# Attention with top-32 selection and an MLP on one core: engines of small copies and the planner's priorities chosen anew

## The chip, the cores and the metric

The kernel runs on one NeuronCore of a Trainium2 chip. The metric is the time of one execution on the device, in microseconds (us), as the median of several runs. The core has five engines with a queue of instructions each: TensorE (PE, matmuls; its weight loads are shown as PEld), VectorE (DVE), ScalarE (ACT), GpSimd (POOL) and SyncE (SP), which here issues all DMAs. An instruction waits in its queue until the semaphores it names have been reached, and what stands behind it waits too.

## The reference

Four batches of eight heads attend over 576 positions; of each row of scores only the 32 largest are kept. The result, as 2304 rows of 512, goes through a matmul to 2048, softplus, and a matmul back to 512.

```python
scores = scale * np.matmul(q, k.transpose(0, 1, 3, 2))
kth = np.partition(scores, -top_k, axis=-1)[..., -top_k:-top_k + 1]
scores = np.where(scores >= kth, scores, -1000000000.0)
attn = softmax(scores)                       # with 1e-09 added to the sum
x = np.matmul(attn, v)                       # heads side by side: 2304 x 512
h = x @ w_in                                 # 512 x 2048
g = np.maximum(h, 0.0) + np.log1p(np.exp(-np.abs(h)))
out = g @ w_out                              # 2048 x 512
```

`w_in` and `w_out` come as 64-bit floats. The kernel splits each of them on the chip into a high and a low float32 part, and runs the matmuls of the MLP with three products (high x high, high x low, low x high).

## The kernel before

**Work and stages.** Heads go in pairs. A batch is cut into two ranges of 256 rows and a remainder of 64 (two heads' remainders share a tile). A step of the sequence is a head pair of one range: for each of two tiles of 128 rows, scores by TensorE (`qk`, line 582), a copy from PSUM by ScalarE (`copy`, lines 680 and 695), then the selection: maxima of eight chunks (`c8`, line 623), three rounds of maxima (`m8`, lines 632 and 638), a count of what lies above (`cnt` on VectorE, line 654, or `sign` and `relu` on ScalarE, lines 648 and 651), products by POOL (`z`, lines 657 and 660) and a last maximum (`w8`, line 662). Then the exponential (`exp`, line 720), the mask with its sum (`mask`, line 723), transposes (`T`, line 738), their copies (`evac`, line 743) and attention times v (`av`, line 783). At the end of a step the row factors are spread out to a tile `rr` (`WIDES`: line 800 on VectorE, 797 on ScalarE, 794 on POOL), and the result is split into a high and a low part x (`xh` on ScalarE, line 822, or `xsplit` on POOL, lines 825 and 828; `X_HIGHS`).

**The MLP** (called MoE in the names) runs over nine blocks of 256 rows, each when its range is done (the remainders of all batches make the ninth), in eight units of two feature tiles. A unit is 24 matmuls of line 915 in PSUM (`moeh`), |h| (line 928), exponential and logarithm on ScalarE (934, 936), the addition on VectorE (`g`, line 942) or on POOL (`gs`, line 939, with a Relu on ScalarE before it), the high part of g (ScalarE, `gh`, line 945, or POOL, `gs`, line 948; `HIGHS`), the low part on POOL (`gs`, line 950) and 12 matmuls of line 960 (`moeo`). The low part of w_in lies in DRAM and is loaded for each tile (`wl`); `wl` is also the class of the output's stores.

**Weights** are prepared in 32 pieces of 128 x 512 in eight parts of four (a part of w_in, then one of w_out, four times): a load of 512 KB (`wload`) to one of two staging buffers, |w| on ScalarE (lines 432 and 446), four steps on VectorE (434 to 442 for the first 20 pieces, whose temporaries lie in PSUM; 449 to 460 for the others, whose clamp is on POOL or on VectorE by `POOL_CLAMPS`), the high part (ScalarE, line 470, or POOL, line 467, by `POOL_HIGHS`), and the low part on POOL (475 and 486). Only pieces from 20 on look at `POOL_CLAMPS`. Five parts come first in the sequence, parts 5 and 6 ahead of the first unit of the first block of the MoE, part 7 ahead of its fourth. The temporaries of a piece and of a unit come from the same ring `a` of two buffers, which are given out in the order of the program. q and k are split on POOL (`split`, lines 503 and 506), turned on TensorE (`prepT`, line 513) and copied on ScalarE (`prepev`, lines 538 and 566), three stages ahead (`AHEAD`).

**Order.** No queue's order is written out by hand. Each piece of work is an `Op` with an engine, a cost, what it depends on, buffers that it takes or frees, and a priority: its place in the sequence (0 to 72 for the steps, 1.5 more for each unit within the MoE) plus an offset from `OFFS`, chosen by its class and by which of four stages its place falls in (below 5.5, 11.5, 60.5, or above). `Plan.forward` goes through the work in time: of the instructions of an engine whose inputs are planned it takes the one that can start first, and among those that could start at the same time the lowest priority. The queues are filled in the order of the starts so found. The places in the sequence span some 80, so offsets that lie further apart than this rank classes whatever their place.

```python
if k in OFFS:
    prio += OFFS[k][sum(prio >= s for s in STAGES)]
```

Of the kernel before, what the change touches and what calls it, by code (L numbers as in the profile page):

```python
# [16 lines left out]
LOW = -3.0e38  # L17
LARGEST = 3.0e38
COUNTS = tuple(map(int, "101111011111111010000010100000000001000000100000010000000001110001111100"))
POOL_CLAMPS = (0, 1, 11, 12, 13, 16, 22, 27, 28, 29, 30)  # L20
POOL_HIGHS = (16, 20, 27, 28)
AHEAD = 3
WIDES = tuple(map(int, "20200000010022000000011110212002"))
GUARDS = (1,)
SPLITS = tuple(map(int, "000000001101110101101000001010110001001100000101101111100010100111000100"))
REST_LAST = (0, 0, 0, 0)
HIGHS = tuple(map(int, "011101011111001100011000011001100010000010011100110110100010101111111001"))
X_HIGHS = tuple(map(int, "000011101000001000011011000011011100"))
W_AT = (-1, -1, -1, -1, -1, 0, 0, 3)
EARLY_PIECES = 20  # L30
EARLY_PAIRS = 8
# [2 lines left out]
PASSES = 0  # L34
SLOPE = 1.5
STAGES = (5.5, 11.5, 60.5)
OFFS = {"T": (-291.57, -322.01, -530.19, -242.94,),
        "av": (-276.33, -303.72, -359.32, -241.06,),
        "c8": (380.01, 363.38, 650.87, 238.59,),
        "cnt": (459.77, 102.79, 428.38, 267.79,),  # L40
        "copy": (563.64, 134.42, 465.54, 349.87,),
        "evac": (-215.5, 195.29, 114.86, -425.45,),
        "exp": (384.13, 367.5, 654.99, 185.69,),
        "g": (459.85, 106.18, 431.76, 267.87,),
        "gh": (157.89, 1.42, -29.55, 2.84,),
        "gs": (-41.02, 199.82, 518.18, 316.26,),
        "guard": (460.45, 92.47, 425.27, 268.16,),
        "inv": (-313.3, -9.08, 77.16, 53.56,),
        "load": (-308.68, -253.81, -285.11, -120.84,),
        "loadv": (-111.81, -2.43, 0.31, -5.31,),  # L50
        "m8": (464.05, 628.42, 662.54, 681.81,),
        "mask": (-279.8, 144.17, 122.8, -287.92,),
        "moeh": (-110.15, -1.19, 1.29, 0.7,),
        "moeo": (-230.73, -31.51, 4.57, 4.37,),
        "neg": (-358.45, -475.13, -56.27, -387.03,),
        "prepT": (-312.78, -270.79, -357.79, -176.61,),
        "prepev": (-284.19, 126.51, 55.57, -348.47,),
        "qk": (148.36, 42.76, 0.24, 1.21,),
        "rb": (655.1, 219.15, 591.6, 419.43,),
        "relu": (558.22, 134.9, 425.49, 532.22,),  # L60
        "sign": (-317.65, -268.47, -359.67, -138.32,),
        "soft": (-44.66, 199.71, 542.61, 328.67,),
        "split": (-170.82, 264.58, 203.08, -458.5,),
        "w8": (385.5, 675.11, 522.15, 411.57,),
        "wl": (-291.21, -321.65, -529.83, -242.58,),
        "wload": (-241.23, -34.37, -0.49, 20.42,),
        "wprep": (-299.35, -227.01, -273.63, -218.46,),
        "xh": (567.18, 145.59, 586.57, 538.21,),
        "xsplit": (-342.34, -259.25, -284.47, -149.07,),
        "z": (-254.7, -227.33, -283.53, -305.94,)}  # L70
BIG = 2.0 ** 40
TIERS = (2, 6, 8)
CHUNKS = 8
# [73 lines left out]
class Plan:  # L147
# [7 lines left out]
    def add(self, eng, cost, fn, deps=(), acq=(), rel=(), prio=0.0, lat=0.0, k=None, port=False):  # L155
        if k in OFFS:
            prio += OFFS[k][sum(prio >= s for s in STAGES)]
        op = Op(eng, cost, fn, list(deps), list(acq), list(rel), prio, lat, len(self.ops),
                port or eng == "pool")
        self.ops.append(op)  # L160
        return op
# [127 lines left out]
def c_act(n, psum=False, ptr=0):  # L289
    return (120 if psum else 162) + 0.714 * n + 93 * ptr  # L290
# [10 lines left out]
def c_pool(n, scalar=False):  # L301
    return 155 + 0.834 * n if scalar else 150 + 2.15 * n
# [3 lines left out]
def topk_attention_moe(ctx: ExitStack, tc: tile.TileContext, q, k, v, w_in, w_out, out):  # L306
# [83 lines left out]
    def add(*args, **kw):  # L390
        return pl.add(*args, **kw)
# [13 lines left out]
    def prep_weights(part, prio):  # L405

        group, which = divmod(part, 2)
        for j in range(4):
# [13 lines left out]
            def high(st=st):  # L422
                return st.ap().rearrange("p (c t) -> p c t", t=2)[:, :, 1]
# [21 lines left out]
            else:  # L445
                ab = add("act", c_act(512) + 45, lambda high=high, tm=tm: nc.scalar.activation(
                    tm.ap(), high().bitcast(F32), AF.Abs), [ld], acq=[tm], prio=prio, k="wprep")
                if piece in POOL_CLAMPS:
                    a0 = add("pool", c_pool(512, True), lambda tm=tm: nc.gpsimd.tensor_scalar(
# [14 lines left out]
            if fast and piece == EARLY_PIECES - 1:  # L464
                add("dve", 0, lambda: None, last_words[-2:], rel=lent[:1], prio=prio, k="g")
            if piece in POOL_HIGHS:
                oh = add("pool", c_pool(512, True), lambda tm=tm, hi=hi: nc.gpsimd.tensor_scalar(
# [290 lines left out]
    def full_range(b, r, hp, qt, qops, kt, kops, vt, vops, seq, last_k):  # L758
# [32 lines left out]
        wide = lambda: sums.ap()[:, 0:4].unsqueeze(2).to_broadcast([P, 4, D])  # L791
        how = WIDES[next(range_no) % len(WIDES)]
        if how == 2:
# [26 lines left out]
    def split_x(x, src, dep, rel, key, hp, prio):  # L820
        if X_HIGHS[next(x_no) % len(X_HIGHS)]:
            h = add("act", c_act(CH), lambda: nc.scalar.activation(x.ap()[:, 0, :], src(), AF.Copy), dep, acq=[x], prio=prio, k="xh")
        else:
            h = add("pool", c_pool(CH, True),
                    lambda: nc.gpsimd.tensor_scalar(x.ap()[:, 0, :], src(), 1.0, 0.0, op0=OP.mult, op1=OP.add), dep, acq=[x],
                    prio=prio, k="xsplit")
        l = add("pool", c_pool(CH),
                lambda: nc.gpsimd.tensor_tensor(x.ap()[:, 1, :], src(), x.ap()[:, 0, :].bitcast(F32), op=OP.subtract),
                [h], rel=rel, prio=prio, k="xsplit")
        xu.setdefault(key, {})[hp] = (x, [h, l])  # L830
# [63 lines left out]
    def moe(key, seq, first):  # L894
# [4 lines left out]
        for s in range(KF // 2):  # L899
# [41 lines left out]
            else:  # L941
                o4 = add("dve", c_dve(512), lambda hb=hb, ab=ab: nc.vector.scalar_tensor_tensor(  # L942
                    ab.ap(), hb.ap(), 0.0, ab.ap(), op0=OP.max, op1=OP.add), [o3], rel=[hb], prio=prio, k="g")
            if HIGHS[unit % len(HIGHS)] and fast:
                g1 = add("act", c_act(512), lambda ab=ab, gb=gb: nc.scalar.activation(gb.ap()[:, 0, :], ab.ap(), AF.Copy),  # L945
# [176 lines left out]
```

## Time and profile before

| | |
|---|---|
| median of 3 runs | 855.11 us (854.74 to 856.41) |
| profiled execution | 853.7 us, span 851.7 us |
| mean granted TensorE clock | 0.954 of full speed |
| busy: PE, PEld, DVE | 89%, 77%, 82% of the span |
| busy: ACT, POOL | 73%, 72% of the span |

Busy shares are means over the whole span, which has stretches with different limits; so the tables by stretch say more. Matmuls are pipelined, so a busy PE is not PE at its peak. The span is that of the instructions; the execution has 2.0 us beside it.

### The profile page before, as it was taken

The numbers are of one execution on the slowest core, as the hardware profiler recorded it, in microseconds if no ns is written. First come the engines' busy times: TensorE is split into PE (matmuls) and PEld (weight loads), VectorE is DVE, ScalarE is ACT, GpSimd is POOL, SyncE is SP. The second block draws the span as 40 slices with busy tenths as digits, with TensorE's granted clock in tenths as the row PEclk, the third lists the DMA queues.
The fourth block names the chain that finished last, engine by engine and source line by source line (L and its number), as shares of the span: only waits on it lengthen the run. The fifth ranks groups of instructions, "written<-read, shape, count | busy, mean of one in ns | idle before, by whom it ended". The sixth has DMA issues, their size and how long they took to land.

```text
span 851.7 us, 18516 instructions
## 1 busy us (share of the span) xinstructions
PE 757.8 (89%) x5894; PEld 658.9 (77%) x5894; DVE 696.3 (82%) x3095; ACT 620.1 (73%) x1196; POOL 613.5 (72%) x817
## 2 busy tenths in 40 slices
PE   2466558698989999999999999999999999999996
PEld 1354447587879898988798889887988898898885
DVE  4999988989998899888998998899987966855000
ACT  3787668889869985877687858866888688955442
POOL 3786557878879987788897775799878558846341
PEclk9986756899999999999999999999999999999999
DMA  7655344623334322424243224242422151051331
GB/s 223 210 143 184 118 127 131 183 84 115 90 95 112 97 71 76 125 68 115 72 126 82 69 69 123 65 114 80 132 82 63 51 137 49 28 162 55 89 93 42
DMA packets 66763, 88.34 MB, mean 104 GB/s; under 512 B 12640, under 2 KB 37216, under 8 KB 66656
## 3 DMA queue, kind: packets, MB, share of 16 engines
q1 hardware_dynamic: 66656, 87.06, 35.6%
q8 instruction: 49, 0.80, 0.4%
q14 instruction: 58, 0.48, 0.2%
HBM read 68.68 MB, written 8.91 MB: 91 GB/s over the span
## 4 chain that ended last, share of the span: by engine, by line
PE 44%; DVE 24%; POOL 14%; ACT 11%; issue 5%; DMA 1%; ACTq 0%; POOLq 0%; DVEq 0%
PE ps L960 14%; PE ps L915 14%; DVE c L623 6%; PE ps L582 6%; POOL z L660 4%; PE ps L783 4%; PE ps L738 4%; DVE kth L662 3%; DVE sg L654 2%; DVE c L638 2%; DVE l L632 2%; POOL g L950 2%; POOL z L657 2%; POOL hl L506 2%; ACT sg L648 2%
## 5 line engine op out<-in xcount | busy, mean ns | idle before, releaser
L960 PE MATMUL ps<-woh,g 128*128 128x512 f32 x576 | 212.6, 409 | 1.4 <-POOL g L950 1.4
L660 POOL TENSOR_TENSOR z<-s,sg 128x576 f32<-128x576 f32 x144 | 194.8, 1353 | 1.0
L623 DVE MAX8 c<-s 128x8 f32<-128x72 f32 x1152 | 168.2, 219 | 30.9 <-ACT s L680 27.7
L915 PE MATMUL ps<-x,wih 128*128 128x256 f32 x1152 | 176.3, 289 | 1.5 <-DVE a L942 1.4
L915 PEld LDWEIGHTS ps<-x,wih 128*128 128x128 f32 x1152 | 152.6, 191 | 5.3 <-DVE a L942 1.8
L582 PE MATMUL ps<-kt,qt 128*128 128x288 f32 (+2 forms) x672 | 132.5, 325 | 9.8 <-ACT s L680 5.3
L743 ACT ACTIVATE et<-ps 128x512 f32<-128x512 f32 (+1 forms) x208 | 103.4, 497 | 45.5 <-PE ps L738 44.7
L662 DVE MAX8 kth<-z 128x8 f32<-128x584 f32 x144 | 109.8, 762 | 23.3 <-POOL z L660 22.4
L960 PEld LDWEIGHTS ps<-woh,g 128*128 128x128 f32 x576 | 108.7, 189 | 23.3 <-POOL g L950 2.5
L582 PEld LDWEIGHTS ps<-kt,qt 128*128 128x128 f32 x672 | 104.3, 205 | 20.6 <-ACT s L680 8.5
L950 POOL TENSOR_TENSOR g<-a,g 128x512 fp32r<-128x512 f32 x72 | 94.9, 1318 | 33.7 <-ACT g L945 31.9
L960 PE MATMUL ps<-wol,g 128*128 128x512 f32 x288 | 113.8, 395 | 0.0
L657 POOL TENSOR_SCALAR z<-small,stats 128x8 f32<-128x8 f32 x144 | 66.0, 458 | 63.4 <-DVE kth L662 29.3
L680 ACT ACTIVATE s<-ps 128x576 f32<-128x576 f32 x128 | 83.2, 650 | 29.0 <-PE ps L582 22.2
L738 PE MATMUL ps<-identr,em 128*128 128x128 f32 x392 | 73.5, 299 | 32.7 <-DVE em L723 17.2
L915 PE MATMUL ps<-x,wil 128*128 128x256 f32 x576 | 95.0, 287 | 0.0
L783 PE MATMUL ps<-et,vt 128*64 128x128 f32 x1280 | 91.6, 294 | 0.0
L738 PEld LDWEIGHTS ps<-identr,em 128*128 128x128 f32 x392 | 50.3, 151 | 46.3 <-ACT et L743 11.0
L783 PEld LDWEIGHTS ps<-et,vt 128*64 128x64 f32 x1280 | 75.1, 146 | 12.6 <-issue 6.8
L915 PEld LDWEIGHTS ps<-x,wil 128*128 128x128 f32 x576 | 78.3, 190 | 0.5 <-issue 0.2
L632 DVE MAX8 l<-c 128x8 f32<-128x64 f32 (+2 forms) x432 | 75.1, 197 | 2.7
L513 PE MATMUL ps<-identr,hl 128*128 128x128 f32 x288 | 40.9, 264 | 35.9 <-POOL hl L506 22.6
(102 smaller groups left out, 1461.1 us busy)
## 6 DMA issues: line engine op xcount, KB each, us to landing
wil<-wil_d SPq DMA_DIRECT2D x144, 256.0 KB, 2.9
qt<-qt SPq DMA_DIRECT2D x72, 128.0 KB, 2.7
shared<-in_moe_w_in_dram SPq DMA_DIRECT2D x16, 512.0 KB, 3.7
shared<-in_moe_w_out_dram SPq DMA_DIRECT2D x16, 512.0 KB, 3.6
nat<-in_q_dram SPq DMA_DIRECT2D x32, 128.0 KB, 2.2
nat<-in_k_dram SPq DMA_DIRECT2D x32, 128.0 KB, 2.2
vt<-in_v_dram SPq DMA_DIRECT2D x16, 256.0 KB, 2.8
wil_d<-g SPq DMA_DIRECT2D x16, 256.0 KB, 2.6
```

Of the source, the lines that this page charges most:

```text
L582: nc.tensor.matmul(sp.ap()[:, c:c + w], qt.ap()[:, a, ti, :], kt.ap()[:, kc:kc + w], start=(a == 0), stop=(a == 1))
L623: nc.vector.max(out=ct[i].ap()[:, 8 * c:8 * c + 8], in_=v[:, c, :])
L632: last[i] = add("dve", c_max(w * CHUNKS), lambda i=i, rnd=rnd, part=part: nc.vector.max(out=lt.ap()[:, i, rnd, :], in_=part(i)), [last[i]] ...
L660: b = add("pool", 150 + 1.92 * S, lambda i=i, sg=sg, z=z: nc.gpsimd.tensor_tensor(z.ap()[:, 0:S], sc[i].ap(), sg.ap(), op=OP.mult), [f], r ...
L662: w = add("dve", c_max(S + 8), lambda z=z, top8=top8: nc.vector.max(out=kth[:, top8:top8 + 8], in_=z.ap()), [b, *order8], rel=[z], prio=pr ...
L680: lambda i=i, sp=sp: nc.scalar.activation(sc[i].ap(), sp.ap(), AF.Copy, scale=scale),
L738: nc.tensor.transpose(tr.ap()[:, j * P:(j + 1) * P], em.ap()[:, c0 + j * P:c0 + (j + 1) * P], ident)
L743: lambda: nc.scalar.activation(et.ap()[:, b0:b0 + n, :].rearrange("p a c -> p (a c)"), tr.ap()[:, 0:n * P], AF.Copy),
L783: nc.tensor.matmul(o[hh * D:(hh + 1) * D, :], vt.ap()[:, hh * NT + j if j < NT else 2 * NT + hh, :], et.ap()[:, hh * NT + j if j < NT else ...
L915: nc.tensor.matmul(o, w, units[kk][0].ap()[:, c, :], start=(n == 0 and kk == 0), stop=(n == 2 and kk == KD - 1))
L950: g2 = add("pool", c_pool(512), lambda ab=ab, gb=gb: nc.gpsimd.tensor_tensor(gb.ap()[:, 1, :], ab.ap(), gb.ap()[:, 0, :].bitcast(F32), op= ...
L960: nc.tensor.matmul(o, gb.ap()[:, a, c:c + P], w[:, f, :], start=(f == 0 and n == 0), stop=(f == KF - 1 and n == 2))
```

## The change

Five tuples that choose engines and the whole table of offsets get new values; no function changes. The choices take effect as follows (counts of the whole program):

| | before | after |
|---|---|---|
| clamps on POOL (pieces 20 to 31) | 22, 27, 28, 29, 30 | 22, 27, 28, 29, 31 |
| high parts of weights on POOL | 16, 20, 27, 28 | 1, 3, 4, 9, 10, 11, 20, 27, 28 |
| row factors on VectorE, ScalarE, POOL | 19, 6, 7 | 17, 7, 8 |
| high parts of g on ScalarE, POOL | 37, 35 | 41, 31 |
| high parts of x on ScalarE, POOL | 14, 22 | 16, 20 |

```diff
-POOL_CLAMPS = (0, 1, 11, 12, 13, 16, 22, 27, 28, 29, 30)
-POOL_HIGHS = (16, 20, 27, 28)
+POOL_CLAMPS = (22, 27, 28, 29, 31)
+POOL_HIGHS = (1, 3, 4, 9, 10, 11, 20, 27, 28)
-WIDES = tuple(map(int, "20200000010022000000011110212002"))
+WIDES = tuple(map(int, "20100020021001201022022000011010"))
-HIGHS = tuple(map(int, "011101011111001100011000011001100010000010011100110110100010101111111001"))
-X_HIGHS = tuple(map(int, "000011101000001000011011000011011100"))
+HIGHS = tuple(map(int, "011111011111001101111000011101110111001010010001000110001111010011010110"))
+X_HIGHS = tuple(map(int, "000011001010101000110011001101111000"))
...
-        "T": (-291.57, -322.01, -530.19, -242.94,),
-        "av": (-276.33, -303.72, -359.32, -241.06,),
-        "c8": (380.01, 363.38, 650.87, 238.59,),
-        "cnt": (459.77, 102.79, 428.38, 267.79,),
-        "copy": (563.64, 134.42, 465.54, 349.87,),
-        "g": (459.85, 106.18, 431.76, 267.87,),
-        "gh": (157.89, 1.42, -29.55, 2.84,),
-        "gs": (-41.02, 199.82, 518.18, 316.26,),
-        "inv": (-313.3, -9.08, 77.16, 53.56,),
-        "load": (-308.68, -253.81, -285.11, -120.84,),
-        "m8": (464.05, 628.42, 662.54, 681.81,),
-        "mask": (-279.8, 144.17, 122.8, -287.92,),
-        "moeh": (-110.15, -1.19, 1.29, 0.7,),
-        "moeo": (-230.73, -31.51, 4.57, 4.37,),
-        "prepT": (-312.78, -270.79, -357.79, -176.61,),
-        "qk": (148.36, 42.76, 0.24, 1.21,),
-        "sign": (-317.65, -268.47, -359.67, -138.32,),
-        "split": (-170.82, 264.58, 203.08, -458.5,),
-        "w8": (385.5, 675.11, 522.15, 411.57,),
-        "wl": (-291.21, -321.65, -529.83, -242.58,),
-        "wload": (-241.23, -34.37, -0.49, 20.42,),
-        "wprep": (-299.35, -227.01, -273.63, -218.46,),
-        "z": (-254.7, -227.33, -283.53, -305.94,)}
+        "T": (-324.15, -345.9, -530.65, -319.11,),
+        "av": (-283.14, -289.79, -359.32, -240.73,),
+        "c8": (406.4, 359.15, 653.29, 262.28,),
+        "cnt": (521.83, 10.31, 421.74, 347.32,),
+        "copy": (580.5, 206.37, 407.71, 326.96,),
+        "g": (536.69, 125.2, 439.85, 385.76,),
+        "gh": (-323.83, -332.81, -365.08, -317.16,),
+        "gs": (440.87, 44.94, 326.47, 178.74,),
+        "inv": (36.81, -88.7, 1.71, -2.55,),
+        "load": (-329.04, -335.29, -359.72, -311.3,),
+        "m8": (524.23, 619.11, 683.88, 660.36,),
+        "mask": (437.66, 81.52, 333.44, 239.57,),
+        "moeh": (-90.39, -42.08, 1.41, 0.85,),
+        "moeo": (-233.07, -22.11, 4.55, 5.15,),
+        "prepT": (-338.79, -273.83, -357.71, -180.91,),
+        "qk": (38.7, -114.5, 0.19, 1.72,),
+        "sign": (-303.77, -237.88, -269.33, -166.3,),
+        "split": (508.2, 71.67, 403.94, 306.36,),
+        "w8": (437.85, 661.49, 450.91, 377.0,),
+        "wl": (-312.15, -449.72, 1.58, -357.77,),
+        "wload": (-1.83, -106.33, -125.62, -70.92,),
+        "wprep": (-299.76, -225.91, -284.63, -249.65,),
+        "z": (-308.89, -226.26, -272.88, -254.56,)}
...
```

The classes left out (`evac`, `exp`, `guard`, `loadv`, `neg`, `prepev`, `rb`, `relu`, `soft`, `xh`, `xsplit`) get new values too.

## Rows read from the trace of the kernel before

**Rows 1.** The head of the profile's page.
```profile
span 851.7 us, 18516 instructions
```

**Rows 2.** Busy time by stretch (from:to, length, engines with counts, granted clock, DMA).
```profile
core 0: us, PE busy (x) PEld busy (x) DVE busy (x) ACT busy (x) POOL busy (x), PEclk, DMA share, GB/s
...
25.00:125.00 100.00, 57.09 (x327) 44.77 (x328) 96.91 (x376) 73.33 (x141) 69.96 (x104) 0.74 0.54 163
125.00:200.00 75.00, 58.97 (x463) 50.58 (x461) 67.11 (x267) 63.45 (x125) 57.41 (x65) 0.86 0.44 132
200.00:675.00 475.00, 464.79 (x3835) 408.52 (x3835) 439.05 (x2073) 364.42 (x709) 383.24 (x526) 1.00 0.32 89
675.00:800.00 125.00, 124.31 (x963) 109.54 (x963) 75.90 (x315) 88.46 (x172) 78.81 (x93) 1.00 0.29 81
800.00:845.00 45.00, 44.84 (x285) 39.76 (x283) 3.46 (x5) 20.08 (x34) 15.77 (x14) 1.00 0.32 90
```

**Rows 3.** Busy time up to 200 us, of line 915 and then of line 960.
```profile
0.00:200.00 200.00, 18.95 (x120) 17.33 (x120) 0.82 0.52 156
...
0.00:200.00 200.00, 9.86 (x36) 6.37 (x36) 0.82 0.52 156
```

**Rows 4.** The chain of work that ended last (start, us, what), near its end.
```profile
825.32 2.80 PE ps L960 x12
828.12 2.80 PE ps L915 x24
```

**Rows 5.** VectorE's waits, 200 to 675 us (total, times, longest).
```profile
DVE c L623 <- ACT s L680: 11.2, 8, 3.2
DVE kth L662 <- POOL z L660: 9.1, 16, 2.1
```

**Rows 6.** Timeline 120 to 174 us (start, us, engine, line): TensorE, POOL, ScalarE, VectorE, TensorE.
```profile
140.68 1.73 PE L915 MATMUL ps<-x,wih 128*128 128x256 f32 x8
...
160.20 1.60 POOL L475 TENSOR_TENSOR g<-a,wih 128x512 fp32r<-128x512 f32 x1
...
162.33 0.58 ACT L928 ACTIVATE a<-ps 128x512 f32<-128x512 f32 x1
...
162.28 0.81 DVE L723 SCALAR_TENSOR_TENSOR em<-s,kth,em 128x576 f32<-128x576 f32 x1
...
172.22 0.48 PE L960 MATMUL ps<-woh,g 128*128 128x512 f32 x1
```

**Rows 7.** Timeline 44 to 57 us: one weight piece, and the load that follows it.
```profile
44.81 0.33 SPq L397 DMA_DIRECT2D shared<-in_moe_w_in_dram  x1
...
50.09 0.65 ACT L432 ACTIVATE ps<-shared 128x512 f32<-128x512 f32 x1
...
54.78 0.67 DVE L442 SCALAR_TENSOR_TENSOR a<-shared,ps 128x512 uint32<-128x512 uint32 x1
...
56.30 0.46 SPq L397 DMA_DIRECT2D shared<-in_moe_w_in_dram  x1
```

**Rows 8.** Groups by line (count, busy us, mean ns, idle before): copies that change engines.
```profile
L470 ACT ACTIVATE wih<-a 128x512 fp32r<-128x512 f32 x14 | 8.8, 629 | 11.1 <-DVE a L442 10.4 <-DVE a L460 0.6
...
L467 POOL TENSOR_SCALAR woh<-a 128x512 fp32r<-128x512 f32 x2 | 1.3, 670 | 2.3 <-DVE a L460 2.3
...
L945 ACT ACTIVATE g<-a 128x512 fp32r<-128x512 f32 x37 | 23.3, 630 | 10.6 <-PE ps L960 5.6 <-POOL a L939 3.7 <-DVE a L942 1.1
...
L948 POOL TENSOR_SCALAR g<-a 128x512 fp32r<-128x512 f32 x35 | 21.8, 623 | 10.2 <-PE ps L960 6.8 <-DVE a L942 2.4 <-PE ps L513 0.5
...
L800 DVE COPY rr<-sum 128x256 f32<-128x256 f32 x19 | 8.3, 436 | 0.1
```

**Rows 9.** Groups by line: the MoE's additions and low parts on POOL.
```profile
L950 POOL TENSOR_TENSOR g<-a,g 128x512 fp32r<-128x512 f32 x72 | 94.9, 1318 | 33.7 <-ACT g L945 31.9
...
L939 POOL TENSOR_TENSOR a<-shared,a 128x512 f32<-128x512 f32 x30 | 39.2, 1308 | 25.6 <-ACT a L936 25.5
```

**Rows 10.** VectorE steps of weight pieces: line 454 (ns min/median/max), line 436 (as rows 8).
```profile
L454 DVE TENSOR_SCALAR a<-a x12: 409/423/1417, 116.1 to 200.0; 128x512 uint32<-128x512 uint32 x12
...
L436 DVE TENSOR_SCALAR ps<-ps 128x512 uint32<-128x512 uint32 x20 | 13.8, 691 | 0.1
```

More of the change, by code (lines that the diff above doesn't have):

```diff
@@ L36 @@
 STAGES = (5.5, 11.5, 60.5)
-OFFS = {"T": (-291.57, -322.01, -530.19, -242.94,),
-        "av": (-276.33, -303.72, -359.32, -241.06,),
-        "c8": (380.01, 363.38, 650.87, 238.59,),
-        "cnt": (459.77, 102.79, 428.38, 267.79,),
-        "copy": (563.64, 134.42, 465.54, 349.87,),
-        "evac": (-215.5, 195.29, 114.86, -425.45,),
-        "exp": (384.13, 367.5, 654.99, 185.69,),
-        "g": (459.85, 106.18, 431.76, 267.87,),
-        "gh": (157.89, 1.42, -29.55, 2.84,),
-        "gs": (-41.02, 199.82, 518.18, 316.26,),
-        "guard": (460.45, 92.47, 425.27, 268.16,),
-        "inv": (-313.3, -9.08, 77.16, 53.56,),
-        "load": (-308.68, -253.81, -285.11, -120.84,),
-        "loadv": (-111.81, -2.43, 0.31, -5.31,),
-        "m8": (464.05, 628.42, 662.54, 681.81,),
-        "mask": (-279.8, 144.17, 122.8, -287.92,),
-        "moeh": (-110.15, -1.19, 1.29, 0.7,),
-        "moeo": (-230.73, -31.51, 4.57, 4.37,),
-        "neg": (-358.45, -475.13, -56.27, -387.03,),
-        "prepT": (-312.78, -270.79, -357.79, -176.61,),
-        "prepev": (-284.19, 126.51, 55.57, -348.47,),
-        "qk": (148.36, 42.76, 0.24, 1.21,),
-        "rb": (655.1, 219.15, 591.6, 419.43,),
-        "relu": (558.22, 134.9, 425.49, 532.22,),
-        "sign": (-317.65, -268.47, -359.67, -138.32,),
-        "soft": (-44.66, 199.71, 542.61, 328.67,),
-        "split": (-170.82, 264.58, 203.08, -458.5,),
-        "w8": (385.5, 675.11, 522.15, 411.57,),
-        "wl": (-291.21, -321.65, -529.83, -242.58,),
-        "wload": (-241.23, -34.37, -0.49, 20.42,),
-        "wprep": (-299.35, -227.01, -273.63, -218.46,),
-        "xh": (567.18, 145.59, 586.57, 538.21,),
-        "xsplit": (-342.34, -259.25, -284.47, -149.07,),
-        "z": (-254.7, -227.33, -283.53, -305.94,)}
@@ new lines @@
+OFFS = {"T": (-324.15, -345.9, -530.65, -319.11,),
+        "av": (-283.14, -289.79, -359.32, -240.73,),
+        "c8": (406.4, 359.15, 653.29, 262.28,),
+        "cnt": (521.83, 10.31, 421.74, 347.32,),
+        "copy": (580.5, 206.37, 407.71, 326.96,),
+        "evac": (-193.99, 216.59, 63.92, -437.06,),
+        "exp": (319.52, 363.16, 721.52, 184.84,),
+        "g": (536.69, 125.2, 439.85, 385.76,),
+        "gh": (-323.83, -332.81, -365.08, -317.16,),
+        "gs": (440.87, 44.94, 326.47, 178.74,),
+        "guard": (1.22, -144.33, -13.98, 25.92,),
+        "inv": (36.81, -88.7, 1.71, -2.55,),
+        "load": (-329.04, -335.29, -359.72, -311.3,),
+        "loadv": (475.88, 82.77, 353.11, 217.11,),
+        "m8": (524.23, 619.11, 683.88, 660.36,),
+        "mask": (437.66, 81.52, 333.44, 239.57,),
+        "moeh": (-90.39, -42.08, 1.41, 0.85,),
+        "moeo": (-233.07, -22.11, 4.55, 5.15,),
+        "neg": (-321.23, -484.49, -18.09, -311.87,),
+        "prepT": (-338.79, -273.83, -357.71, -180.91,),
+        "prepev": (7.86, -43.1, 64.37, 33.81,),
+        "qk": (38.7, -114.5, 0.19, 1.72,),
+        "rb": (603.54, 239.36, 666.58, 472.35,),
+        "relu": (602.35, 107.29, 388.15, 537.0,),
+        "sign": (-303.77, -237.88, -269.33, -166.3,),
+        "soft": (-62.58, 234.2, 580.81, 317.04,),
+        "split": (508.2, 71.67, 403.94, 306.36,),
[3 more added lines that the diff above has]
+        "wprep": (-299.76, -225.91, -284.63, -249.65,),
+        "xh": (547.37, 123.93, 616.24, 613.36,),
+        "xsplit": (-296.71, -231.74, -269.12, -231.45,),
+        "z": (-308.89, -226.26, -272.88, -254.56,)}
```

## The prediction

> **What bounds the kernel now.** I read the stretches first. The table of busy time by stretch has three parts [rows 2]. From 25 to 125 us VectorE is busy 96.91 of 100 us and TensorE 57.09, at a granted clock of 0.74: the start belongs to VectorE, which does the top-32 search and the bit work on the weights at once. From 200 to 675 us both are nearly full, TensorE 464.79 and VectorE 439.05 of 475 us, at clock 1.00. From 675 on TensorE is alone: 124.31 of 125 us and 44.84 of 45, while VectorE falls to 75.90 and 3.46. The span is 851.7 us [rows 1].
>
> So the end is set by TensorE's backlog of MoE matmuls. In the last steps a MoE unit takes 2.80 us for 12 matmuls of line 960 and 2.80 us for 24 of line 915 [rows 4]. That is 0.233 us and 0.117 us each, so 864 and 1728 of them (9 blocks of 16 feature tiles, 6 and 12 matmuls per tile) come to 201.6 us each, 403 us together. Before 200 us only 36 and 120 have run [rows 3], 8.4 + 14.0 = 22.4 us. The other 381 us must fit behind 200 us, beside attention. A microsecond by which the MoE starts earlier, or a TensorE hole closed after 200 us, is worth up to a microsecond at the end. The visible holes there are 475 - 464.79 = 10.2 us, 0.7 us and 0.2 us [rows 2], 11 in all (a few more inside busy time, since a busy TensorE is not TensorE at peak).
>
> Why does the MoE start late? The first matmuls of line 915 run at 140.68 us, the first of line 960 only at 172.22 [rows 6]. Between them, `ab`, the first unit's |h| on ScalarE (line 928), waits until 162.33, although its matmuls were long done. Its buffer comes from ring `a`, two buffers taken in program order, and the weight pieces of parts 5 and 6 stand ahead of it. It starts 0.5 us after the POOL subtraction of a weight piece ends (160.20 + 1.60 = 161.80). The weight chain, 28 of 32 pieces of it, is the gate. One step of it [rows 7]: load issued at 44.81, |w| on ScalarE at 50.09, last VectorE step 54.78 to 55.45, and the next load at 56.30. Two staging buffers, 11.5 us a round, so 5.7 us a piece.
>
> **The change part by part.** No instruction is added or removed; engines of some copies change, and the planner's priorities, from which the order on every queue follows. I compared the priorities inside each engine and stage (offset plus sequence number, lower first).
>
> *Late clamps.* Pieces below 20 never read the tuple, so of 11 entries before only 22, 27, 28, 29 and 30 acted, and now 31 stands for 30. Zero: one piece of part 7 for another, both past the gate.
>
> *High parts of the weights.* On POOL were 16, 20, 27, 28; now 1, 3, 4, 9, 10, 11, 20, 27, 28. Five more at 0.670 us (line 467) for five fewer on ScalarE at 0.629 us [rows 8]: 3.4 us on POOL for 3.1 us on ScalarE, all in early pieces. The copy is not in the two-buffer round: the next load follows the last VectorE step [rows 7]. So most of it is hidden by the load's wait of 5 us; it shows only where ScalarE held the next |w| behind a copy that waited for VectorE. Ends -3.1 and +3.4 us (all of either on the chain); I take -1.0, nearer to zero because of the cover. If the load were short, the whole 3.1 would show.
>
> A trace row speaks against POOL: the VectorE step of line 454, both operands in SBUF, takes 409 ns at best and 1417 at worst [rows 10], while the step of line 436, whose temporary lies in PSUM, averages 691.
> The Trainium skill, "SBUF — State Buffer", section "Who interferes with whom", says that VectorE in a two-port mode and GpSimd exclude each other for a whole instruction; by it five more POOL copies would cost up to five blocks. It exempts VectorE operations with at most one SBUF input outside these modes.
> The pieces moved are early ones, whose steps use PSUM; so I leave this at zero in the sum, and as a rival below.
>
> *MoE copies and row factors.* The high parts of g: 41 instead of 37 on ScalarE, 4 x 0.630 = 2.5 us more there and 4 x 0.623 = 2.5 us less on POOL [rows 8]. Of x two more go to ScalarE. Row factors on VectorE fall from 19 to 17, 2 x 0.436 = 0.87 us less [rows 8]; one more each on ScalarE and POOL. ScalarE and POOL end within about 1 us of where they were, which the 23% and 19% idle of both from 200 to 675 us hides [rows 2]. VectorE's part: -0.9 to +0.4 (one copy's worth, if the new engine delivers later); I take -0.5.
>
> *Order before 11.5 (the first eleven steps of the sequence).* TensorE: in the second stage qk's offset goes from 42.76 to -114.5, ahead of the MoE matmuls (-22 and -42), where it stood behind. VectorE: masks go behind c8 in the first stage; in the second g (line 942) goes behind masks. ScalarE: `gh` now goes first. POOL: in the first stage `split` (k, q) goes last but one and z ahead of the weights. SP: loads stay ahead of weights, so no queue of DMAs is overtaken by another. qk earlier can fill VectorE's 75 - 67.11 = 7.9 us of idle from 125 to 200 us at most [rows 2]; g behind one mask (0.81 us [rows 6]) in two units costs 1.6 us, because the unit's PSUM buffer is freed by g and TensorE's next unit waits for it. Ends -7.9 and +1.6; I take -1.0, because the gate of ring `a` is not moved by qk, so that TensorE can use only little of what VectorE gains.
>
> *Order from 11.5 to 60.5 (the bulk).* On TensorE all offsets stay within 0.5 (T, then av and prepT, then qk and MoE); on VectorE the ranking inv, mask, cnt, g, w8, c8, m8 is the same. What changes is on the feeders: ScalarE takes gh, before sign, and POOL takes the MoE's gs (518 to 326) before split (203 to 404). Output stores and wil loads (`wl`) go behind the loads and weights on SP. What could be won is VectorE's wait for copies, 11.2 us, and for z, 9.1 us [rows 5], 20 us, but TensorE's holes cap it at 10.2. What could be lost: a split now waits behind a unit's three POOL operations, 1.308 + 0.623 + 1.318 = 3.25 us [rows 8, 9]. Ends -10.2 and +9.8 (3.25 at each of the three later batches). I take -2.0: a fifth of the holes, since both full engines keep their order and only feeders move.
>
> *Order from 60.5.* TensorE is full (0.9 us of holes), its order is kept, and what VectorE, ScalarE and POOL do earlier meets a full queue. Zero, ends -0.9 and +1.
>
> Sum: -1.0 - 0.5 - 1.0 - 2.0 = -4.5 us. The profiled execution took 853.7 us (span 851.7 plus 2.0 around it), so 849.2; its time lies 1.4 us under the median of the runs, 855.1, so 850.6 for the median.
>
> **The rivals.** *Nothing moves.* The full engines keep their order in the bulk, the weight gate stays at 162 us, and every term is hidden: 855, within 853.4 and 856.8. For it speaks that engine sums change by under 1 us; against it that 26 of the 72 g copies change engines and all early orders are new. That the clamp part hardly does what it says belongs here.
>
> *A closer weave.* If the early part brings the gate forward by about 4 us (0.3 us in each of 14 rounds, out of 5 us between load and |w|) and the bulk closes all 10.2 us of holes, 855.1 - 14 = 841. Against it: the waits are spread over many causes.
>
> *Slower: split starved.* `split` makes k and q for stages three ahead. Put behind gs, it decides once POOL has no pause longer than gs leaves between z's; POOL is busy 383 of 475 us [rows 2], so pauses exist, but z comes first as well. Then qk has no operands at a batch's start, VectorE's c8 waits, and nothing makes it up: 3 x 3.25 = 9.8 us, 865; with half of it hidden, 860.
>
> *The port.* Five POOL copies each block VectorE for their 0.670 us in the stretch where it is 97% busy: +3.4, and with the gains of the bulk missing, 858.5.
> The Trainium skill, "SBUF — State Buffer", section "Who interferes with whom", is the rule behind it.
>
> **How the numbers follow.** Forecast of -4.5 (own range 845 to 853.4): 0.42. Closer weave (under 845): 0.18. Nothing: 0.18. Split starved: 0.17. Port: 0.05. Predicted 850.6. From 841 to 860 leaves out half of the closer weave's chance and about half of the starved case's, under 0.2. Faster by over 0.2% (1.7 us, about what a measurement of this kernel can tell from no change): 0.42 + 0.18 = 0.60; within it 0.18; slower 0.17 + 0.05 = 0.22.
>
> **What would show it.** Gate: the first ScalarE operation of line 928 at 161 to 163 us; earlier by 3 us or more is the closer weave. Bulk: TensorE busy over 467 of 475 us, VectorE's wait for copies and z under 20 us. Split starved: TensorE or ScalarE waiting for line 506 after 200 us, VectorE's wait for copies over 20 us. Port: lines 454 and 457 slower on average. End: TensorE full from 675 us to the last matmul; if it has holes there, the reading that its backlog sets the end is wrong.

## The result, and the profile after

| | before | after |
|---|---|---|
| median of 4 runs | 855.76 us (854.74 to 856.69) | 847.17 us (845.87 to 848.72) |
| ratio | 1 | 0.9906 (95%: 0.9892 to 0.992) |
| profiled execution | 853.7 us | 848.72 us |

The changed kernel is 8.6 us faster; 850.6 was forecast, in a range from 841 to 860. The two profiled executions lie 5.0 us apart (4.8 us in their spans), since the one of after is the longest of its four runs and the one of before lies 1.0 us under the shortest of its four. So the traces can account for 5.0 of the 8.6 us.

Busy time after in three stretches, as in [rows 2]:

```profile
125.00:200.00 75.00, 60.08 (x463) 52.15 (x461) 68.69 (x274) 63.43 (x125) 56.33 (x66) 0.81 0.44 132
200.00:675.00 475.00, 468.32 (x3881) 412.75 (x3882) 438.82 (x2079) 372.95 (x722) 381.61 (x521) 1.00 0.33 90
675.00:800.00 125.00, 124.38 (x953) 110.31 (x952) 70.81 (x299) 86.80 (x171) 78.48 (x92) 1.00 0.30 84
```

From 200 to 675 us TensorE is busy 3.5 us longer than in [rows 2], while VectorE is where it was (438.82 against 439.05). By 200 us both kernels have run the same 120 matmuls of line 915 and 36 of line 960, so the start gave TensorE nothing. VectorE is a little further: from 125 to 200 us it ran 274 instructions instead of 267, 1.6 us more. Up to 200 us, as in [rows 3]:

```profile
0.00:200.00 200.00, 18.91 (x120) 16.76 (x120) 0.77 0.52 156
...
0.00:200.00 200.00, 9.53 (x36) 6.32 (x36) 0.77 0.52 156
```

To see where the lead is made, the same matmul has to be found in both runs. The chain of work that ended last passes the same groups of lines 915, 783 and 960 in both. Before:

```profile
690.21 1.41 PE ps L915 x12
691.62 1.24 PE ps L783 x20
...
836.52 8.41 PE ps L960 x36
```

After:

```profile
685.65 1.40 PE ps L915 x12
687.05 1.24 PE ps L783 x20
...
831.84 8.41 PE ps L960 x36
```

The lead is 4.56 us at the first of these groups, 4.57 us at the second, which belongs to attention, and 4.68 us at the last. So nearly all of it is made before 690 us, and attention is as far ahead as the MoE. From 200 us up to the first of these groups both kernels have run the same 3994 matmuls; before, then after:

```profile
200.00:690.21 490.21, 479.32 (x3994) 422.15 (x3995) 449.18 (x2101) 376.21 (x733) 395.13 (x539) 1.00 0.32 90
```

```profile
200.00:685.65 485.65, 478.66 (x3994) 422.51 (x3995) 444.55 (x2092) 380.59 (x738) 391.79 (x534) 1.00 0.33 91
```

TensorE's holes are 10.9 us in the one and 7.0 us in the other, so 3.9 of the 4.6 us are closed holes; the other 0.7 us is less busy time for the same matmuls. VectorE's holes are 41.0 and 41.1 us, so it waits no less; it is busy 4.6 us less, 444.55 against 449.18, with 9 instructions fewer to run, for some were done before 200 us. No run tells whether TensorE's holes closed because VectorE was quicker, or on their own.

The two largest of TensorE's waits from 200 to 675 us before, then the largest after (total, times, longest):

```profile
PE ps L738 <- ACT et L743: 3.5, 6, 0.7
PE ps L513 <- POOL hl L506: 1.8, 1, 1.8
```

```profile
PE ps L738 <- ACT et L743: 1.7, 2, 0.9
```

The wait for line 506 is gone after, the one for line 743 is halved, and some smaller ones are new.

A count of matmuls at fixed times misleads here. By 675 us after is ahead by 21 matmuls of line 915 (1061 against 1040), worth 2.5 us at 0.117 us each. From 675 to 800 us it runs 17 more of them (400 against 383), but 27 fewer of other lines, since the totals are 953 and 963: by then it has less attention left, and gains no more.

So on TensorE the gain is holes closed between 200 and 690 us, and attention and the MoE come forward alike. VectorE's waits from 200 to 675 us, as in [rows 5], did not shrink:

```profile
DVE c L623 <- ACT s L680: 14.9, 12, 3.1
DVE kth L662 <- POOL z L660: 10.5, 12, 4.0
```

The gate of the MoE, as in [rows 6], on TensorE, POOL and ScalarE:

```profile
140.99 2.02 PE L915 MATMUL ps<-x,wih 128*128 128x256 f32 x8
...
158.67 1.27 POOL L475 TENSOR_TENSOR g<-a,wih 128x512 fp32r<-128x512 f32 x1
...
160.41 0.59 ACT L928 ACTIVATE a<-ps 128x512 f32<-128x512 f32 x1
```

Again |h| of the first unit starts as the subtraction of a weight piece ends, 0.5 us after it, 1.9 us sooner than before. And the groups that answer to [rows 8] and [rows 10]:

```profile
L945 ACT ACTIVATE g<-a 128x512 fp32r<-128x512 f32 x41 | 25.8, 628 | 12.3 <-POOL a L939 3.8 <-DVE a L942 3.5 <-PE ps L960 3.5
L948 POOL TENSOR_SCALAR g<-a 128x512 fp32r<-128x512 f32 x31 | 21.1, 680 | 16.6 <-PE ps L960 11.0 <-DVE a L942 2.6 <-PE ps L738 2.5
L800 DVE COPY rr<-sum 128x256 f32<-128x256 f32 x17 | 8.8, 516 | 0.1
L436 DVE TENSOR_SCALAR ps<-ps 128x512 uint32<-128x512 uint32 x20 | 13.8, 691 | 0.1
...
L454 DVE TENSOR_SCALAR a<-a x12: 406/418/846, 116.1 to 200.3; 128x512 uint32<-128x512 uint32 x12
```

The copies moved as counted. The two row factors fewer on VectorE saved nothing there: 17 copies took 8.8 us, 19 had taken 8.3. Their median fell from 337 to 296 ns, but the longest rose from 796 to 1274 ns. It started while POOL ran a product of line 660, and ended 0.1 us after it:

```profile
177.62 1.29 POOL L660 TENSOR_TENSOR z<-s,sg 128x576 f32<-128x576 f32 x1
...
177.78 1.27 DVE L800 COPY rr<-sum 128x256 f32<-128x256 f32 x1
```

### The profile page after: what moved, and what is told of

It is laid out like the page before. It is cut to its first block, busy times and chain, and to the rows that moved or that the text cites. A ratio compares the mean times of both kernels' runs of the same rounds, so it can differ in the third digit from the quotient of the medians.

```text
span 846.9 us, 18504 instructions
## 1 busy us (share of the span) xinstructions
PE 761.0 (90%) x5894; PEld 663.5 (78%) x5894; DVE 692.4 (82%) x3093; ACT 621.6 (73%) x1198; POOL 613.2 (72%) x817
## 4 chain that ended last, share of the span: by engine, by line
PE 46%; DVE 35%; ACT 9%; POOL 6%; issue 4%; DMA 0%; ACTq 0%; POOLq 0%; DVEq 0%
PE ps L960 14%; PE ps L915 14%; DVE c L623 8%; PE ps L582 5%; PE ps L738 5%; PE ps L783 5%; DVE kth L662 4%; DVE em L723 4%; DVE sg L654 3%; DVE c L638 3%; DVE l L632 2%; POOL z L660 2%; DVE shared L723 2%; DVE ps L439 1%; DVE ps L434 1%
## 5 line engine op out<-in xcount | busy, mean ns | idle before, releaser
L660 POOL TENSOR_TENSOR z<-s,sg 128x576 f32<-128x576 f32 x144 | 192.6, 1338 | 0.7
L662 DVE MAX8 kth<-z 128x8 f32<-128x584 f32 x144 | 109.6, 761 | 25.8 <-POOL z L660 25.1
L582 PEld LDWEIGHTS ps<-kt,qt 128*128 128x128 f32 x672 | 106.4, 209 | 19.7 <-ACT s L695 7.1
L657 POOL TENSOR_SCALAR z<-small,stats 128x8 f32<-128x8 f32 x144 | 67.9, 471 | 62.3 <-DVE kth L662 24.8
L738 PE MATMUL ps<-identr,em 128*128 128x128 f32 x392 | 75.7, 306 | 36.5 <-DVE em L723 20.0
L654 DVE TENSOR_SCALAR_CACHE_REDUCE sg<-s,l 128x576 bf16<-128x576 f32 x90 | 71.6, 804 | 0.4
```

The source lines that it names most:

```text
L582: nc.tensor.matmul(sp.ap()[:, c:c + w], qt.ap()[:, a, ti, :], kt.ap()[:, kc:kc + w], start=(a == 0), stop=(a == 1))
L654: a = add("dve", c_dve(S, 1), lambda i=i, sg=sg, st=st: nc.vector.tensor_scalar(sg.ap(), sc[i].ap(), lt.ap()[:, i, 2, 7:8], None, op0=OP.i ...
L660: b = add("pool", 150 + 1.92 * S, lambda i=i, sg=sg, z=z: nc.gpsimd.tensor_tensor(z.ap()[:, 0:S], sc[i].ap(), sg.ap(), op=OP.mult), [f], r ...
L662: w = add("dve", c_max(S + 8), lambda z=z, top8=top8: nc.vector.max(out=kth[:, top8:top8 + 8], in_=z.ap()), [b, *order8], rel=[z], prio=pr ...
L738: nc.tensor.transpose(tr.ap()[:, j * P:(j + 1) * P], em.ap()[:, c0 + j * P:c0 + (j + 1) * P], ident)
```

## The experiments

Three theories went in. **A**: the parts of the change add up, each by its own cost, and the order of the feeders in the bulk carries the gain. **B**: the new engines carry it. **C**: neither; any change of a number makes the planner write another plan for everything behind it, and that moves the time by some us at random. Medians are given with the ratio to the kernel before in the same runs.

### The parts by themselves

Engines alone, the five tuples of the change with the old offsets:

```diff
-POOL_HIGHS = (16, 20, 27, 28)
+POOL_HIGHS = (1, 3, 4, 9, 10, 11, 20, 27, 28)
...
```

> The kernel before with the five tuples of the change (engines of clamps, high parts, row factors) and the old offsets. Theory A (the gain is one of order on the feeders in the bulk): 853 to 858, within 0.3% of before, since the sums of the engines move by under 1 us. Theory B (the gain is in the engines, above all four g copies and two row factors taken off POOL and VectorE): 847 to 850. Theory C (any new plan moves the time by some us at random): anything from 849 to 862.

Measured: 871.18 us, 1.0184 (1.0165 to 1.0203). Slower by 16 us.

All offsets alone, with the old tuples:

```diff
-        "qk": (148.36, 42.76, 0.24, 1.21,),
+        "qk": (38.7, -114.5, 0.19, 1.72,),
...
```

> The kernel before with all new offsets and the old tuples. Theory A (order): 846 to 850, nearly the whole gain of 8.6 us. Theory B (engines): 853 to 858. Theory C (any new plan moves the time at random): no relation to the changed kernel, 845 to 862.

Measured: 875.27 us, 1.0247 (1.0223 to 1.0272).

The third column of the offsets alone:

```diff
-        "gs": (-41.02, 199.82, 518.18, 316.26,),
+        "gs": (-41.02, 199.82, 326.47, 316.26,),
...
```

> The kernel before with new offsets in the third stage alone (places 11.5 to 60.5). Theory A (order of the feeders in the bulk): 847 to 851, TensorE busy over 467 of 475 us from 200 to 675 us. If the gain comes from the early stages or the last one: 854 to 857, TensorE busy about 465 there.

Measured: 872.38 us, 1.0189 (1.0169 to 1.0208).

The first two columns alone:

```diff
-        "qk": (148.36, 42.76, 0.24, 1.21,),
+        "qk": (38.7, -114.5, 0.24, 1.21,),
...
```

> The kernel before with new offsets in the first two stages alone (places below 11.5). Theory A (bulk): 853 to 857, the first operation of line 928 at 161 to 163 us. If qk ahead of the first MoE matmuls matters: 850 to 853, with VectorE busier than 68 of 75 us from 125 to 200 us. Masks behind c8 and g behind masks could also cost: up to 859.

Measured: 871.38 us, 1.0179 (1.0159 to 1.0198).

Each half costs 16 to 20 us, and the columns 16 and 17; the whole gives 8.6 back. All four lie above every range that was named for them, that of C too, which ended at 862. Theory A as I had it, a sum of parts, falls with these four, and so does B as an explanation of the gain. Two readings were left: the new engines and the new order need each other, or whatever differs from a chosen set is slow (C in a new form: both kernels' plans are uncommonly good ones).

### Engines against plans

To part the engines from the plan, the next kernels plan the order (and all buffers) with one set of tuples and issue the instructions on the engines of the other. The two sets differ in 63 choices: 26 high parts of g, 10 of x, 18 row factors, 7 high parts of weights and 2 clamps (the expectation below says 46).

New engines in the order planned for the old ones:

```diff
+RUN_HIGHS = tuple(map(int, "011111011111001101111000011101110111001010010001000110001111010011010110"))
...
+            if RUN_HIGHS[unit % len(HIGHS)] and fast:
+                g_high = lambda ab=ab, gb=gb: nc.scalar.activation(gb.ap()[:, 0, :], ab.ap(), AF.Copy)
...
             if HIGHS[unit % len(HIGHS)] and fast:
-                g1 = add("act", c_act(512), lambda ab=ab, gb=gb: nc.scalar.activation(gb.ap()[:, 0, :], ab.ap(), AF.Copy),
-                         [o4], acq=[gb], prio=prio, k="gh")
...
+                g1 = add("act", c_act(512), g_high, [o4], acq=[gb], prio=prio, k="gh")
...
```

> The order of all work is planned with the old tuples and offsets, as in the kernel before; only then the instructions are issued on the engines of the new tuples (46 engine choices differ or so). Theory A (engines matter by their sums alone, under 1 us): 853 to 859. Theory B (the mixes of the first four runs were slow because the new engines cost time by themselves): 868 to 874. Theory C (what costs is a plan whose parameters were not chosen together; here the plan is the old one): 853 to 859, with the loss of 15 us of the kernel with new engines and old offsets gone.

Measured: 860.59 us, 1.0062 (1.0047 to 1.0077), 1.6 us above the range of A and C and far under that of B. Of the 16 us that the new engines cost with the old offsets, 5 remain when the plan is the old one; 11 came from the plan that was written for them.

The other way round, the changed kernel's plan with the engines of before (the same edit, `RUN_` tuples with the old values):

```diff
+RUN_HIGHS = tuple(map(int, "011101011111001100011000011001100010000010011100110110100010101111111001"))
...
```

> The order is planned as in the changed kernel, with its tuples and offsets; the instructions are issued on the engines of the old tuples. If the whole gain is in the order that the new plan writes: 846 to 850. If the engines carry it: 853 to 857.

Measured: 856.06 us, 1.0006 (0.9996 to 1.0015). The new order with the old engines gives nothing. By the expectation this would say that the engines carry the gain, but the same engines cost 5 us in the old plan; only the two together are faster. TensorE's busy time from 200 to 800 us, for the changed kernel, this one, the kernel before and the one with new engines in the old plan, in that order (each line is of another kernel, each with the columns of [rows 2]):

```profile
200.00:800.00 600.00, 592.71 (x4832) 523.06 (x4833) 509.63 (x2377) 459.74 (x892) 460.08 (x613) 1.00 0.32 89
```

```profile
200.00:800.00 600.00, 587.83 (x4778) 515.92 (x4778) 512.43 (x2380) 453.92 (x878) 461.44 (x615) 1.00 0.31 88
```

```profile
200.00:800.00 600.00, 589.10 (x4795) 518.06 (x4796) 514.95 (x2386) 452.89 (x881) 462.06 (x619) 1.00 0.31 88
```

```profile
200.00:800.00 600.00, 585.61 (x4742) 513.78 (x4743) 516.30 (x2385) 455.23 (x885) 460.27 (x615) 0.99 0.31 88
```

Against the plan's own engines, the old ones open 4.9 us of holes on TensorE in the new plan, and the new ones 3.5 us in the old plan. So the gain belongs to neither part alone; in these four kernels an order fits the engines it was planned for.

### One clamp

The smallest part of the change, the first tuple, of which one entry acts:

```diff
-POOL_CLAMPS = (0, 1, 11, 12, 13, 16, 22, 27, 28, 29, 30)
+POOL_CLAMPS = (22, 27, 28, 29, 31)
```

> The kernel before with the first tuple of the change alone, of which only the clamp of piece 31 instead of piece 30 on POOL takes effect. Theory A (parts add up, each by its own cost): 854 to 857, as one 0.7 us clamp stands for another. Theory C (any change of a parameter rewrites the whole plan, and the plans of the kernel before and of the changed kernel are both picked ones): 868 to 880; the planner's own span for this plan is 864.8 us, against 841.9 before and 838.9 after.

Measured: 881.40 us, 1.0308 (1.0294 to 1.0322), 1.4 us above the range of C: 25.8 us for one operation of 0.7 us that changes places with its twin.

The same two clamps, issued on the new engines in the order planned with the old tuple:

```diff
+RUN_POOL_CLAMPS = (22, 27, 28, 29, 31)
...
+                if piece in RUN_POOL_CLAMPS:
...
```

> The same two clamps change engines, but in the order planned with the old tuple. All theories but one expect 854 to 857; over 860 would say that the clamp itself costs, and not the order.

Measured: 855.75 us, 1.0006 (0.9995 to 1.0017). The clamps themselves cost nothing that can be measured; the 25.8 us are the plan.

The swap undone in the changed kernel:

```diff
-POOL_CLAMPS = (22, 27, 28, 29, 31)
+POOL_CLAMPS = (0, 1, 11, 12, 13, 16, 22, 27, 28, 29, 30)
```

> The changed kernel with the old tuple of clamps, so that the clamp of piece 30 instead of piece 31 is on POOL. Theory A (parts add up): 846 to 849. Theory C (any change rewrites the plan, and the plan, not the engine of the clamp, sets the time): 869 to 879; the planner's own span for it is 861.2 us. Then the same swap would cost about 25 us from either side, though it is done in opposite directions.

Measured: 880.62 us, 1.0298 (1.0284 to 1.0312), 33 us above the changed kernel and 1.6 us above the range of C. The same swap in opposite directions costs 26 us from one side and 33 from the other, as theory C has it, though with more than the 25 it named.

Where do they go? In the kernel with one clamp the first |h| of the MoE still starts at 162.5 us, and 120 and 36 matmuls are done at 200 us, as before. Then it falls behind; its profiled execution is 27.7 us longer than that of before. Its busy time from 200 to 800 us and from 750 us, then what is left after 800 us of line 915 and of line 960:

```profile
200.00:800.00 600.00, 574.73 (x4609) 503.90 (x4610) 516.83 (x2377) 445.85 (x862) 448.35 (x609) 0.97 0.31 85
750.00:800.00 50.00, 43.43 (x298) 37.95 (x298) 31.48 (x123) 27.44 (x52) 29.16 (x37) 0.90 0.25 70
...
800.00:880.00 80.00, 32.96 (x264) 31.80 (x262) 0.99 0.28 78
...
800.00:880.00 80.00, 39.17 (x156) 28.18 (x156) 0.99 0.28 78
```

The same two of before:

```profile
800.00:880.00 80.00, 23.25 (x189) 22.59 (x187) 0.97 0.20 58
...
800.00:880.00 80.00, 23.38 (x96) 17.59 (x96) 0.97 0.20 58
```

Left are 264 and 156 matmuls instead of 189 and 96: 75 x 0.117 + 60 x 0.233 = 22.8 us of work. Two things put it off. TensorE's holes from 200 to 800 us are 25.3 us instead of 10.9, 14.4 us more, and no single wait holds them: the largest one between 200 and 675 us is 7.2 us in 11 pieces. And the granted clock from 200 to 800 us is 0.97 of full speed instead of 1.00. It fell near 440, 600, 625 and 780 us: from 438 to 445, 598 to 602, 622 to 629 and 776 to 786 us it was 0.51 to 0.57, and TensorE busy 21.2 of these 28 us. If half of that is lost, the clock costs some 10 us, an estimate, and both together are 24 of the 27.7 us.

In the changed kernel with the old clamps the stretch from 750 us is worse:

```profile
750.00:800.00 50.00, 38.41 (x239) 34.15 (x240) 20.84 (x71) 20.32 (x39) 20.80 (x24) 0.80 0.21 64
```

### Is it chance, or does the planner know?

The planner reckons a span for each plan that it writes. For the kernels above whose engines and plan belong together it is 841.9 us before, 838.9 after, and 852.1 to 864.8 for the six mixtures, so it foresaw that these are poor. Moving one high part of g or of x to the other engine (108 plans from each kernel) gives reckoned spans with quartiles of 841.9, 851.3 and 858.2 us from the kernel before, and 838.9, 843.0 and 850.9 from the changed one; 42 of 108 stay within 1 us of their start in both cases, and the best are 841.1 and 838.7. Both kernels stand at low points of a rough ground.

So three more sets of values were looked for with that reckoned span as the only guide. The first:

```diff
-HIGHS = tuple(map(int, "011101011111001100011000011001100010000010011100110110100010101111111001"))
+HIGHS = tuple(map(int, "011110110101010011101100000100110111001000011001100011101100010000000001"))
...
```

> Other values for the same five tuples and offsets, for which the kernel's own planner reckons a span of 834.6 us (before 841.9, changed kernel 838.9). If the planner's span is a fair guide (it stood 8 to 20 us under the measured time in seven plans so far): 843 to 852, near the changed kernel or below it. If the changed kernel's 847 owes to chance on the chip beyond the planner: 850 to 856. TensorE's holes from 200 to 800 us should be under 8 us in the first case and over 10 in the second.

Measured: 853.11 us, 0.9974 (0.9964 to 0.9985).

The second:

```diff
-X_HIGHS = tuple(map(int, "000011101000001000011011000011011100"))
+X_HIGHS = tuple(map(int, "010011101000100010100110110111110010"))
...
```

> A second, independent set of values of the same tuples and offsets; the planner reckons 834.9 us. If the planner's span is a fair guide: 843 to 852; if chance beyond it decides: 850 to 856.

Measured: 854.75 us, 0.9992 (0.9982 to 1.0003).

The third, reached from the kernel before:

```diff
-WIDES = tuple(map(int, "20200000010022000000011110212002"))
+WIDES = tuple(map(int, "10200000021011200112000110001212"))
...
```

> A third set of values, reached from those of the kernel before; the planner reckons 837.6 us, 1.3 us under the changed kernel. If the planner's span is a fair guide: 846 to 855; the same rule of holes.

Measured: 860.51 us, 1.0063 (1.005 to 1.0077). All three missed the expectation that the planner's span is a fair guide down to some us; none beats the changed kernel. The first two lie in the range named for chance beyond the planner (850 to 856), and TensorE's holes from 200 to 800 us are over 10 us in all three, as was expected for that case. All kernels, by measured time, with what orders them roughly, TensorE's busy time:

| kernel | reckoned by the planner | measured | difference | TensorE busy, 200 to 800 us |
|---|---|---|---|---|
| changed | 838.9 | 847.2 | 8.3 | 592.71 |
| first new set | 834.6 | 853.1 | 18.5 | 588.70 |
| second new set | 834.9 | 854.8 | 19.9 | 586.93 |
| before | 841.9 | 855.8 | 13.9 | 589.10 |
| clamp, old plan | 841.9 | 855.8 | 13.9 | 587.91 |
| old engines, new plan | 838.9 | 856.1 | 17.2 | 587.83 |
| third new set | 837.6 | 860.5 | 22.9 | 583.06 |
| new engines, old plan | 841.9 | 860.6 | 18.7 | 585.61 |
| engines alone | 855.2 | 871.2 | 16.0 | 578.31 |
| first two columns | 852.1 | 871.4 | 19.3 | 578.86 |
| third column | 857.8 | 872.4 | 14.6 | 577.66 |
| all offsets | 855.4 | 875.3 | 19.9 | 575.53 |
| changed, old clamps | 861.2 | 880.6 | 19.4 | 571.29 |
| one clamp | 864.8 | 881.4 | 16.6 | 574.73 |

The planner parts good plans from poor ones (under 842 from over 852, measured under 861 from over 871), but inside the good group its order is not the chip's. The measured time stands 14 to 23 us above the reckoned one everywhere but in the changed kernel, where it is 8.3. Of the gain of 8.6 us the planner reckoned 3.0; the other 5.6 us are a better agreement of plan and chip. The two traces show only 1.8 us of this (spans of 851.7 and 846.9 us, reckoned 841.9 and 838.9), and why this plan agrees better stays open. Putting the old engines into it takes all 8.9 us away again, which fits, but names no mechanism.

## Why the prediction was right, and where it was not

**What bounds the kernel: right.** TensorE's MoE backlog sets the end. Over all kernels the time goes roughly with TensorE's holes after 200 us (the table above). Closed holes of TensorE account for 3.9 us of the lead of 4.7 us that after has at the end; with one clamp the added holes are 14.4 of 27.7 us, and the clock adds to them, which the prediction had left out. TensorE was full from 675 us, as foreseen, and over 467 of 475 us in the bulk.

**The gate: right.** |h| started at 160.41 us, just outside the 161 to 163 named, and less than 3 us earlier; by 200 us it had brought no matmul. So the terms of the start (high parts -1.0, early order -1.0, row factors -0.5) had brought TensorE nothing by then, and the row factors did not even shorten VectorE's copies. The 7 instructions that VectorE was ahead may be part of what the bulk gained later; that is not shown.

**The bulk: right place, wrong source, too small.** I took -2.0 us, by VectorE waiting less for copies and z. Those waits rose from 20.3 to 25.4 us. What closed were holes of TensorE, 3.9 us of them, and the lead at 690 us is 4.6 us.

**From place 60.5: right.** I priced it at zero. From 690 us to the end the lead grows by 0.1 us, from 4.56 to 4.68.

**The sum itself: right in its total, not in its making.** The step that does not hold is "I compared the priorities inside each engine and stage" and priced each change of rank by itself. The planner takes what can start first and uses ranks only for ties, so one changed duration early shifts everything behind it. The late clamps, priced at zero, cost 25.8 us alone; the bounds of the bulk, -10.2 to +9.8, were passed by its column alone, +17. That the whole stayed within the range is due to the two kernels both being good plans, which no row of before showed. The parts gave me no ground for a size, so its being near was luck: 2.5 of the 4.5 us were expected from the start, which gave TensorE nothing by 200 us, and the lead made after it is more than twice the bulk's term.

**The rivals.** *Nothing moves*: no. *Closer weave*: its mechanism, holes closed in the bulk, is what happened, at 847 instead of 841, and without the earlier gate. *Split starved*: no; line 506 does not appear among TensorE's waits after 200 us, where before it had 1.8 us. *The port*: not where it was looked for. Lines 454 and 457 became faster on average (533 to 458 and 833 to 809 ns), and the worst case of line 454 fell from 1417 to 846 ns. A copy of line 800 was held up to 1274 ns beside POOL, but by a product and not by a high part. Line 436 stays at 691 ns beside five more POOL copies. The rule of the Trainium skill, "SBUF — State Buffer", section "Who interferes with whom", exempts steps with at most one SBUF input outside the two-port modes, and for the early pieces the trace agrees.

## What to carry to other kernels

Where a program writes the order of the queues, a change of any number is a change of the whole order: price the plan, not the part, and look first at how much one-number neighbours scatter (here up to 26 and 33 us on the chip, against a gain of 8.6). To learn what an engine choice costs by itself, keep the order and change only the engine. Compare two plans by when the same matmul runs in each: a lead read at a few such places tells where it was made, while a count at a fixed time mixes it with the order in the queue.

## What the runs showed of the hardware that was not expected

A TensorE short of work in a late stretch also loses clock, so that a hole there costs more than its length. In the changed kernel with the old clamps the granted clock was 0.80 of full speed from 750 to 800 us, a mixture of the levels 2.4 and 1.2 GHz, where TensorE was busy 38.41 of 50 us. Read in steps of 5 us, it was 0.50 to 0.55 from 755 to 765 us and from 775 to 785 us. Before the first of these TensorE had been busy 2.60 of 5 us, before the second 3.67 of 5 us. In the second it waited 5.4 us for VectorE's line 1042: the plan had put the kernel's closing test of its selection (line 1048) ahead of MoE matmuls. Twenty matmuls of line 783 at the full clock and at the lower one:

```profile
738.08 1.31 PE L783 MATMUL ps<-et,vt 128*64 128x128 f32 x20
...
759.02 2.40 PE L783 MATMUL ps<-et,vt 128*64 128x128 f32 x20 [2.83 <-DVE rb L816]
```

TensorE was busy 12.2 us in these two places. If half of that is lost, the clock cost some 6 us there, an estimate, beside 11.6 us of holes from 750 to 800 us. With one clamp the clock was 0.90 at 43.43 us. Before and after it was 1.00 there, at 49.99 and 49.90 us.
